# The tokens of an inverse 47-point transform as 64x47 products on four quarters of TensorE, in place of 128x94 products on the whole array

## The chip, the cores and the metric

The kernel runs on one core of one Trainium2 chip. The metric is the device time of one execution in microseconds (us). Three runs of the kernel before took 2612.84 to 2614.05 us, with a median of 2612.94 us. The profiled execution is another one, of 2617.29 us; its span, which every view below is read against, is 2615.5 us.

## The reference

Eight sequences of 3008 rows by 256 channels go through a real Fourier transform along the rows, a complex linear layer with bias, a soft threshold, and the inverse transform. The 24064 resulting rows ("tokens") go through a feed-forward network of 256 to 2048 to 256 channels with a sigmoid-gated activation.

```python
X = np.fft.rfft(x, axis=1)
Yr = Xr @ w_r - Xi @ w_i + b_r
Yi = Xr @ w_i + Xi @ w_r + b_i
Yr = np.sign(Yr) * np.maximum(np.abs(Yr) - lam, 0.0)
Yi = np.sign(Yi) * np.maximum(np.abs(Yi) - lam, 0.0)
y = np.fft.irfft(Yr + 1j * Yi, n=x.shape[1], axis=1)
...
h = x @ w_in
g = h * (1.0 / (1.0 + np.exp(-1.702 * h)))
return (g @ w_out).astype(np.float32)
```

## The kernel before

The length 3008 is 64 x 47, so each transform is done as products with a 64-point and a 47-point matrix. For one sequence, `dft47` (or `stage_a`) applies the 47-point step, `dft64` (in `stage_b`) the 64-point step, `stage_mix` the linear layer, `threshold` the soft threshold, and `stage_inv` the inverse 64-point step. The result lies in DRAM as the tile `s2`, of shape [48, 2, 32, 256]: 24 frequencies times real and imaginary part, then `p` (0 or 1: even and odd rows of the transform), then 32 columns `j`, then 256 channels.

What is left is the inverse 47-point step, and this is what the change touches. `load_u(u)` (L525) brings two columns `j` of `s2` into an SBUF tile `ur` of 96 partitions: the 48 values of p = 0 and the 48 of p = 1 lie interleaved in the partitions. `tokens(u)` (L533) multiplies it: the stationary operand is a 96x128 piece of `ur` (one column, one half of the channels), the moving operand is the constant `kz`, 96x94. `kz` holds the 47-point matrix twice, once for each p, with zeros where the p of the row and the p of the column differ. Four products (two columns, two channel halves) fill one PSUM tile `pa` with 2 x 188 columns: 188 tokens by 256 channels. `split` (L147) then writes it out twice: ScalarE casts it to a rounded high part `th`, and VectorE subtracts this from the PSUM tile to get the low part `tl`. There are 16 such groups for a sequence, 128 in all. A tile `th`, `tl` holds 512 tokens; a group that crosses a border of 512 is split in two pieces.

All these products are FP32. TensorE carries each out as two pairs of a weight load and a matmul, so the 512 products of `tokens` stand as 1024 weight loads and 1024 matmuls in the trace. The products of the feed-forward network are in a rounded format (fp32r), where each factor is a high and a low part and three products stand for one (`mm3`, L156): each of those is one load and one matmul.

The feed-forward network takes 512 tokens at a time (47 blocks). `Ffn.up(q)` makes the hidden values of 256 of the 2048 units (12 matmuls of 128x512), `down(q)` the output sums (21 matmuls of 128x256, a seven-product scheme), each over eight values of q. While the blocks run, the spectral steps of the next sequences are emitted between them in step with a cost count, and `tokens_to` (L618) emits `tokens` shortly before a block needs them. It loads one group ahead.

A scheduler then orders the instructions of each engine, and each engine takes its own in that order. The buffers that matter here: `bank()` hands out four PSUM tiles `pa`, used by `tokens`, `up`, `dft64`, `stage_mix` and the other spectral steps alike; `buf2` hands out seven SBUF tiles under one tag, used by `ur` and by nearly all intermediate tiles of the spectral steps and of the output. DMA starts of these tiles are issued on the queue of SyncE (SP).

One more place of the kernel before matters for reading the trace: in the first sequence, `stage_inv` (inside `first_batch`) multiplies with stationary operands on 64 partitions, those of i = 0 on partitions 0 to 63 and those of i = 1 on partitions 64 to 127, each 64x128, with 256 moving columns and an output tile `pi` for each i:

```python
for r in range(2):
    for i in range(2):
        hs = slice(64 * i, 64 * i + 64)
        mm(po[i][:, h], st[r][hs], v[hs, r], start=r == 0, stop=r == 1)
```

Of the kernel before, what the change touches and what calls it, by code (L numbers as in the profile page):

```python
# [9 lines left out]
F32 = mybir.dt.float32  # L10
# [9 lines left out]
S, N1, N2 = 3008, 64, 47  # L20
D, DFF = 256, 2048
LAM = 0.01
NS = 24
NJ = N1 // 2
JP = 2 * 2 * N2
NU = NJ // 2
TOK, HT = 512, 256
NQ = DFF // 256
W2 = 7
WARM = 3  # L30
PK, PKR = 618, 822
TINY = float(np.uint32(897 << 20).view(np.float32))


# [5 lines left out]
def halves(v):  # L40

    def r12(u):
        m, e = np.frexp(u)
        return np.ldexp(np.rint(m * 4096.0), e - 12)

    hi = r12(v)
    return hi, r12(v - hi)


def constants():  # L50
    def ang(a, b, n):
        return 2.0 * np.pi * ((np.outer(a, b)) % n) / n

    n1, n2, k1, k2 = np.arange(N1), np.arange(N2), np.arange(N1), np.arange(NS)
    t47 = ang(n2, k2, N2)
    t64 = ang(n1, k1, N1)


    fa = np.zeros((48, NS, 2))
    fa[:N2, :, 0] = np.cos(t47)  # L60
    fa[:N2, :, 1] = -np.sin(t47)
    a = np.kron(fa.reshape(48, 48), np.eye(2))


    sign = np.ones((N1, NS))
    for kk2 in range(1, NS):
        for kk1 in range(N1):
            k = next(k for k in range(kk2, S, N2) if k % N1 == kk1)
            sign[kk1, kk2] = 1.0 if k <= S // 2 else -1.0


    c, s = np.cos(t64), np.sin(t64)
    b = np.stack([np.block([[c, -s * sign[:, k]], [s, c * sign[:, k]]]) for k in range(NS)])
    b = b.reshape(NS // 2, 2, 2 * N1, 2 * N1).transpose(0, 2, 1, 3)


    w0r, w0i = np.zeros(N1), np.zeros(N1)
    for kk1 in range(N1):
        if next(k for k in range(0, S, N2) if k % N1 == kk1) <= S // 2:
            edge = kk1 in (0, N1 // 2)  # L80
            w0r[kk1] = (1.0 if edge else 2.0) / S
            w0i[kk1] = 0.0 if edge else 2.0 / S
    ct, st = c.T, s.T
    inv = np.block([[ct, st], [-st, ct]])
    binv = inv * (2.0 / S)
    binv0 = inv * np.concatenate([w0r, w0i])[:, None]
    binv0[:, N1:] = 0.0


    ai = np.zeros((NS, 2, 2, 2, N2))  # L90
    for p in range(2):
        ai[:, 0, p, p] = np.cos(t47.T)
        ai[:, 1, p, p] = -np.sin(t47.T)
    ai = ai.reshape(96, 94)

    packs = np.zeros((128, PKR), np.float32)
    packs[:96, 0:192] = np.concatenate(halves(a), 1)
    packs[:, 192:704] = np.concatenate([h[i] for h in halves(np.stack([binv, binv0])) for i in range(2)], 1)
    packs[:96, 704:798] = ai
    packs[:, 798:822] = 1.0  # L100
    packs[N1:, 798:822] = sign

    kinv = np.stack([binv[:N1], binv[N1:]], 1)
    kfirst = np.concatenate([np.stack([binv0[:N1], binv0[N1:] * sign[:, :1]], 1),
                             np.stack([binv[:N1], binv[N1:] * sign[:, 1:2]], 1)])
    pack = np.zeros((128, PK), np.float32)
    pack[:, 0:256] = np.tile(kinv, (2, 1, 1)).reshape(128, 256)
    pack[:, 256:512] = kfirst.reshape(128, 256)
    pack[:, 512:524] = sign.T.reshape(NS // 2, 2 * N1).T
    pack[:96, 524:618] = ai  # L110
    plain = np.zeros((128, 128), np.float32)
    plain[:96, 0:96] = a
    return np.concatenate([plain, np.eye(128, dtype=np.float32), pack, packs], 1), b.astype(np.float32)
# [3 lines left out]
def fourier_mix_then_gated_ffn(ctx: ExitStack, tc: tile.TileContext, x, w_r, w_i, b_r, b_i, w_in, w_out, pack, kbs, out):  # L117
    nc = tc.nc
    NB = x.shape[0]
    NT = out.shape[0]  # L120
    a96, eye, pack, packs = pack[:96, 0:128], pack[:, 128:256], pack[:, 256:256 + PK], pack[:, 256 + PK:256 + PK + PKR]
# [10 lines left out]
    def bank():  # L132
        return ps_a.tile([128, 512], F32, name="pa", tag="pa")

    def buf(shape, dt, name, tag=None, bufs=2):
        return wk.tile(shape, dt, name=name, tag=tag or name, bufs=bufs)

    def buf2(name):
        return buf([128, 2, D], F32, name, tag="w2", bufs=W2)

    def after(*keys):
        held = ExitStack()
        for k in keys:
            held.enter_context(tc.issue_after(done_at[k]))
        return held

    def split(hi, lo, src):  # L147
        nc.scalar.copy(hi, src)  # L148
        return nc.vector.tensor_tensor(lo, src, hi.bitcast(F32), ALU.subtract)  # L149
# [3 lines left out]
    def mm(ps, w, t, start=True, stop=True):  # L153
        last[0] = nc.tensor.matmul(ps, lhsT=w, rhs=t, start=start, stop=stop).ins  # L154
# [9 lines left out]
    def const(shape, dt, name):  # L164
        return cst.tile(shape, dt, name=name, tag=name.rstrip("_"))

    ka = const([96, 128], F32, "ka")
    ki = const([128, 512], F32, "ki")
    kz = const([96, 94], F32, "kz")
    fg = const([128, NS], F32, "fg")  # L170
    bias = const([128, 2, D], F32, "bias")
    wf = const([128, 3, 2, D], F32, "wf")
# [2 lines left out]
    parts, done_at = {}, {}  # L175
# [9 lines left out]
    def constants_in():  # L185
        nc.sync.dma_start(ki, pack[:, 0:512])
        nc.sync.dma_start(fg[:, 0:12], pack[:, 512:524])
        nc.sync.dma_start(kz, pack[:96, 524:618])
        nc.sync.dma_start(bias[:, 0], b_r.broadcast_to([128, D]))
        nc.sync.dma_start(bias[:, 1], b_i.broadcast_to([128, D]))  # L190
        with after(("w", 0)):
            nc.vector.tensor_scalar(bias, bias, LAM, None, ALU.subtract)
# [7 lines left out]
                nc.vector.scalar_tensor_tensor(wf[:, i], wf[:, 2], -1.0, wi, ALU.mult, op)  # L200

    def rounded_parts():
        pk = buf([128, 822], F32, "pk", tag="sx", bufs=3)
        nc.sync.dma_start(pk, packs)
        parts["a"] = const([96, 2, 96], F32R, "ka_")
        parts["i"] = const([128, 2, 2, 128], F32R, "ki_")
        parts["f"] = const([128, NS], F32, "fg_")
        nc.scalar.copy(parts["a"].rearrange("p a b -> p (a b)"), pk[:96, 0:192])
        nc.scalar.copy(parts["i"].rearrange("p h z n -> p (h z n)"), pk[:, 192:704])
        nc.scalar.copy(parts["f"], pk[:, 798:822])  # L210
        wr, wi = buf2("wr"), buf2("wi")
        for t, w in ((wr, w_r), (wi, w_i)):
            nc.sync.dma_start(t, w.rearrange("(c p) e -> p c e", p=128))
        parts["h"] = const([128, 3, 2, D], F32R, "wf_h")
        parts["l"] = const([128, 3, 2, D], F32R, "wf_")
        split(parts["h"][:, 2], parts["l"][:, 2], wr)
        for i, op in ((0, ALU.add), (1, ALU.subtract)):
            t = buf2("wd")
            nc.vector.scalar_tensor_tensor(t, wr, -1.0, wi, ALU.mult, op)
            split(parts["h"][:, i], parts["l"][:, i], t)  # L220
# [302 lines left out]
    s2s, us, ytiles = {}, {}, {}  # L523

    def load_u(u):  # L525
        b, jp = divmod(u, NU)
        if b < NB and u not in us and b in s2s:
            t = buf2("ur")[:96]
            s2v = s2s[b].rearrange("c p j d -> (c p) j d")
            nc.sync.dma_start(t, s2v[:, 2 * jp:2 * jp + 2])  # L530
            us[u] = t

    def tokens(u):  # L533
        t = us.pop(u)
        pv = bank()[:, :2 * JP].rearrange("p (c n) -> p c n", c=2)
        for c in range(2):
            for j in range(2):
                mm(pv[:, c, 94 * j:94 * j + 94], t[:, j, 128 * c:128 * c + 128], kz)
        lo = JP * u
        while lo < JP * (u + 1):  # L540
            k, at = divmod(lo, TOK)
            n = min(JP * (u + 1) - lo, TOK - at)
            if k not in ytiles:
                ytiles[k] = (fbuf([128, 2, TOK], F32R, "th"), fbuf([128, 2, TOK], F32R, "tl"))
            th, tl = ytiles[k]
            o = lo - JP * u
            split(th[:, :, at:at + n], tl[:, :, at:at + n], pv[:, :, o:o + n])
            lo += n

    def fbuf(shape, dt, name, bufs=2):  # L550
        return ff.tile(shape, dt, name=name, tag=name, bufs=bufs)
# [66 lines left out]
    def tokens_to(n):  # L618
        nonlocal done
        while done < NB * NU and JP * done < n:  # L620
            load_u(done)
            load_u(done + 1)
            tokens(done)
            done += 1
        load_u(done)
# [41 lines left out]
    for q in range(8):  # L667
        with after(("i", 5)):
            dft47(1, q, x1[q // 2][:, 2 * (q % 2):2 * (q % 2) + 2])
        if q == 1:  # L670
            for u in range(3):
                load_u(u)
    for n in (7, 8):
        with after(("v", 11)):
# [23 lines left out]
    for n in range(NT * NQ):  # L698
        k, q = divmod(n, NQ)
# [10 lines left out]
        elif not queue and nextb < NB:  # L710
# [4 lines left out]
            total, spent, n0 = sum(c for c, _ in queue), 0.0, n  # L715
            n1 = NQ * S * nextb // TOK - 12
            nextb += 1
        while queue and spent < total * (n + 1 - n0) / (n1 - n0):
            c, step = queue.pop(0)
# [46 lines left out]
```

## Time and profile before

| | value |
|---|---|
| median of three runs | 2612.94 us |
| the profiled execution | 2617.29 us |
| its span | 2615.5 us |
| ScalarE (ACT) busy | 1635.6 us, 63% |
| VectorE (DVE) busy | 1983.4 us, 76% |
| matmuls of `tokens` (`pa<-kz,ur`) | 1024, first at 105.6 us, last at 2541.3 us |
| weight loads of the whole program | 16711 |
| loads of `ur` from DRAM | 128, 192 KB each, median 3.0 us from issue to landing |
| DMA over the span | 214.16 MB, mean 82 GB/s |

How to read the views. PE is TensorE's matmuls, PEld its weight loads, which run beside matmuls; the recorded duration of a matmul includes its way through the array, so what a matmul costs in a dense stretch is read from the distance between starts, not from its duration. A row of a timeline gives the start in us, the duration in us, the engine, the line, the operation, the output and input tiles, the form of the array (rows*columns in use), the shape of the operand, and how many like instructions were merged. All matmuls go through the helper `mm` and stand at L154, so they are told apart by their tiles. A row of waits gives who waited for whom, the total in us, how often, and the longest.

### The profile page before, as it was taken

To read this page: it belongs to the slowest core of one execution; us is meant where nothing else is said; L and a number is where in the kernel's file an instruction comes from. 1 tells how busy PE (TensorE), PEld (TensorE's weight loads), DVE (VectorE), ACT (ScalarE), POOL (GpSimd) and SP (SyncE) were. 2 spreads that over 40 slices of the span, in tenths; PEclk is the share of its full clock that TensorE was granted. 3 is DMA by queue.
4 is the path that set the end of the run, shared out by engine and by line. 5 is a ranking of instruction groups with operands and counts; after the bars stand their busy time and mean duration, and the time that the engine had idled before them with its cause. 6 is when DMAs were issued, how large, how long until landed. Compare 5 with 4: busy or idle time off the path is not lost. (4 is left out here: it accounts for less than half of the span.)

```text
span 2615.5 us, 42827 instructions
## 1 busy us (share of the span) xinstructions
PE 2585.2 (99%) x16711; PEld 2334.6 (89%) x16711; DVE 1983.4 (76%) x3214; ACT 1635.6 (63%) x2536; POOL 56.8 (2%) x66
## 2 busy tenths in 40 slices
PE   8999999999999999999999999999999999999998
PEld 7669999999899998999989999899998899999997
DVE  6688777787778777787777877777777787777776
ACT  4566665666766667666676666766666566655554
POOL 0000000000000000000000000000000000000000
PEclk9999999999999999999999999999999999999999
DMA  6553331222322224222242222322223132200000
GB/s 189 158 173 91 90 105 56 58 72 61 110 77 74 84 69 129 64 81 81 72 131 65 82 72 82 119 61 84 81 85 116 46 95 74 79 24 26 18 20 17
DMA packets 168396, 214.16 MB, mean 82 GB/s; under 512 B 16368, under 2 KB 119120, under 8 KB 168192
## 3 DMA queue, kind: packets, MB, share of 16 engines
q1 hardware_dynamic: 166144, 204.00, 26.4%
q0 software_dynamic: 2048, 7.41, 1.0%
q8 instruction: 132, 2.16, 0.4%
q14 instruction: 72, 0.59, 0.1%
HBM read 117.49 MB, written 93.85 MB: 81 GB/s over the span
## 5 line engine op out<-in xcount | busy, mean ns | idle before, releaser
L572 ACT ACTIVATE gb<-pa 128x512 f32<-128x512 f32 x752 | 448.3, 597 | 447.9 <-PE pa L154 445.6
L149 DVE TENSOR_TENSOR lt<-gt,ht 128x1024 fp32r<-128x1024 f32 x376 | 465.9, 1239 | 248.9 <-ACT ht L148 248.3
L154 PE MATMUL pa<-th,wi_h 128*128 128x512 f32 x1504 | 593.6, 395 | 0.5 <-ACT th L148 0.5
L154 PE MATMUL pa<-tl,wi_h 128*128 128x512 f32 x1504 | 591.8, 394 | 0.0
L154 PE MATMUL pa<-th,wi_l 128*128 128x512 f32 x1504 | 588.4, 391 | 0.0
L148 ACT CAST ht<-gt 128x1024 fp32r<-128x1024 f32 x376 | 393.8, 1047 | 153.0 <-DVE gt L583 151.9
L154 PE MATMUL po<-lt,wo_h 128*128 128x256 f32 x1504 | 411.8, 286 | 0.6 <-DVE lt L149 0.6
L154 PE MATMUL po<-ht,wo_l 128*128 128x256 f32 x1504 | 407.9, 284 | 0.0
L149 DVE TENSOR_TENSOR lb<-gb,hb 128x768 fp32r<-128x768 f32 x376 | 361.5, 961 | 27.7 <-ACT hb L148 25.0
L581 DVE TENSOR_TENSOR gt<-gb 128x512 f32<-128x512 f32 x376 | 259.3, 690 | 159.6 <-ACT gb L572 152.2
L154 PE MATMUL po<-ht,wo_h 128*128 128x256 f32 x1504 | 360.2, 284 | 1.6 <-ACT ht L148 1.4
L154 PEld LDWEIGHTS pa<-th,wi_l 128*128 128x128 f32 x1504 | 283.7, 189 | 56.3
L148 ACT CAST hb<-gb 128x768 fp32r<-128x768 f32 x376 | 314.4, 836 | 22.8 <-PE po L154 15.6
L154 PEld LDWEIGHTS pa<-th,wi_h 128*128 128x128 f32 x1504 | 284.8, 189 | 44.9 <-ACT th L148 0.7
L154 PEld LDWEIGHTS pa<-tl,wi_h 128*128 128x128 f32 x1504 | 284.9, 189 | 41.1
L154 PE MATMUL po<-lb,wo_h 128*128 128x256 f32 x1128 | 317.9, 285 | 2.1 <-DVE lb L149 2.1
L154 PE MATMUL po<-hb,wo_l 128*128 128x256 f32 x1128 | 315.6, 283 | 0.0
L154 PE MATMUL po<-hb,wo_h 128*128 128x256 f32 x1128 | 313.6, 291 | 0.0
L154 PEld LDWEIGHTS po<-lt,wo_h 128*128 128x128 f32 x1504 | 286.3, 190 | 10.7 <-issue 1.6
L154 PEld LDWEIGHTS po<-ht,wo_l 128*128 128x128 f32 x1504 | 286.1, 191 | 8.6 <-issue 2.5
L154 PEld LDWEIGHTS po<-ht,wo_h 128*128 128x128 f32 x1504 | 262.3, 190 | 11.9 <-ACT ht L148 1.6
L154 PEld LDWEIGHTS po<-lb,wo_h 128*128 128x128 f32 x1128 | 214.3, 190 | 10.4 <-DVE lb L149 2.2
(102 smaller groups left out, 3591.6 us busy)
## 6 DMA issues: line engine op xcount, KB each, us to landing
s<-iev SPq DMA_DIRECT2D x96, 256.0 KB, 2.2
ur<-s SPq DMA_DIRECT2D x128, 192.0 KB, 3.0
out<-o SPq DMA_DIRECT2D x94, 256.0 KB, 2.2
s<-aev SPq DMA_DIRECT2D x112, 192.0 KB, 2.3
br<-s SPq DMA_DIRECT2D x84, 256.0 KB, 3.0
yd<-mv SPq DMA_DIRECT2D x168, 128.0 KB, 2.4
yr<-yd SPq DMA_DIRECT2D x84, 256.0 KB, 3.0
xr<-in_x SPq DMA_DIRECT2D x104, 192.0 KB, 3.1
```

Of the source, the lines that this page charges most:

```text
L148: nc.scalar.copy(hi, src)
L149: return nc.vector.tensor_tensor(lo, src, hi.bitcast(F32), ALU.subtract)
L154: last[0] = nc.tensor.matmul(ps, lhsT=w, rhs=t, start=start, stop=stop).ins
L572: done_at["g"] = nc.scalar.activation(o, ps.rearrange("p (h n) -> p h n", h=2), AF.Gelu_apprx_sigmoid).ins
L581: nc.vector.tensor_tensor(gt[:, 0:2], b12, gb[:, 0:3:2], ALU.subtract)
```

## The change

The two values of p no longer share a product. The constant `kz` becomes the bare 48x47 matrix, held twice, on partitions 0 to 47 and 64 to 111. A group has four columns j in place of two (64 groups in place of 128), and its input is two `ur` tiles, each with two columns; p = 0 lies on partitions 0 to 47 and p = 1 on 64 to 111, so each tile is loaded by two DMAs of 96 KB. A product has a stationary operand of 48 partitions by 64 channels and 47 moving columns; its place in the array follows from the partitions of its input (the half of the rows, p) and of its output (the half of the columns, the channel block c modulo 2). Four products in a row thus lie on the four quarters. A group is 32 products and fills two PSUM tiles, one for each p, of 376 columns. On TensorE the order of the group's products among themselves is fixed by hand. The outputs are written to `th` and `tl` with a stride, since each PSUM tile has runs of 47 tokens that alternate with those of the other one; a column that crosses a border of 512 tokens is written in pieces of its own.

```diff
-JP = 2 * 2 * N2
-NU = NJ // 2
+JP = 4 * 2 * N2
+NU = NJ // 4
...
-    ai = np.zeros((NS, 2, 2, 2, N2))
-    for p in range(2):
-        ai[:, 0, p, p] = np.cos(t47.T)
-        ai[:, 1, p, p] = -np.sin(t47.T)
-    ai = ai.reshape(96, 94)
+    ai = np.stack([np.cos(t47.T), -np.sin(t47.T)], 1).reshape(48, N2)
...
-    kz = const([96, 94], F32, "kz")
+    kz = const([128, N2], F32, "kz")
...
     def load_u(u):
         b, jp = divmod(u, NU)
         if b < NB and u not in us and b in s2s:
-            t = buf2("ur")[:96]
-            s2v = s2s[b].rearrange("c p j d -> (c p) j d")
-            nc.sync.dma_start(t, s2v[:, 2 * jp:2 * jp + 2])
-            us[u] = t
+            s2v = s2s[b].rearrange("c p j d -> p c j d")
+            us[u] = [buf2("ur") for h in range(2)]
+            for h, t in enumerate(us[u]):
+                for p in range(2):
+                    nc.sync.dma_start(t[64 * p:64 * p + 48], s2v[p, :, 4 * jp + 2 * h:4 * jp + 2 * h + 2])
 
     def tokens(u):
-        t = us.pop(u)
-        pv = bank()[:, :2 * JP].rearrange("p (c n) -> p c n", c=2)
-        for c in range(2):
-            for j in range(2):
-                mm(pv[:, c, 94 * j:94 * j + 94], t[:, j, 128 * c:128 * c + 128], kz)
-        lo = JP * u
-        while lo < JP * (u + 1):
-            k, at = divmod(lo, TOK)
-            n = min(JP * (u + 1) - lo, TOK - at)
+        ts = us.pop(u)
+        pv = [bank()[:, :JP].rearrange("p (c j n) -> p c j n", c=2, j=4) for p in range(2)]
+        with tc.manual_schedule(engines={mybir.EngineType.PE}):
+            for j in reversed(range(4)):
+                for c in range(4):
+                    i = 64 * (c % 2)
+                    for p in reversed(range(2)):
+                        hs = slice(64 * p, 64 * p + 48)
+                        mm(pv[p][i:i + 64, c // 2, j], ts[j // 2][hs, j % 2, 64 * c:64 * c + 64], kz[hs])
+        for k in range(JP * u // TOK, (JP * (u + 1) - 1) // TOK + 1):
             if k not in ytiles:
                 ytiles[k] = (fbuf([128, 2, TOK], F32R, "th"), fbuf([128, 2, TOK], F32R, "tl"))
             th, tl = ytiles[k]
-            o = lo - JP * u
-            split(th[:, :, at:at + n], tl[:, :, at:at + n], pv[:, :, o:o + n])
-            lo += n
+            at = [JP * u + 94 * j - TOK * k for j in range(4)]
+            js = [j for j in range(4) if 0 <= at[j] and at[j] + 94 <= TOK]
+            for p in range(2):
+                if js:
+                    hi, lo = (t[:, :, at[js[0]]:at[js[0]] + 94 * len(js)].rearrange("p c (j n) -> p c j n", j=len(js))[:, :, :, 47 * p:47 * p + 47]
+                              for t in (th, tl))
+                    split(hi, lo, pv[p][:, :, js[0]:js[0] + len(js)])
+                for j in range(4):
+                    a = at[j] + 47 * p
+                    n0, n1 = max(0, -a), min(47, TOK - a)
+                    if j not in js and n0 < n1:
+                        split(th[:, :, a + n0:a + n1], tl[:, :, a + n0:a + n1], pv[p][:, :, j, n0:n1])
...
-            for u in range(3):
+            for u in range(2):
                 load_u(u)
```

How the scheduler's order moves is shown at two places. The first is TensorE in the middle of the program, where matmuls of the feed-forward network (`po` of `down`, `pa<-th,wi_h` of `up`) stand around a group of `tokens` (`pa<-kz,ur`); `[waits ...]` names the queues and engines whose semaphores a row waits for. In the kernel before:

```order
L154 MATMUL po_7137<-ht,wo_l 128x256
L154 MATMUL po_7139<-lt,wo_h 128x256
L154 MATMUL pa<-kz,ur 128x94 [waits DMAHW4_49,DVE_49]
L154 MATMUL pa<-kz,ur 128x94 x3
L154 MATMUL po_7139<-ht,wo_l 128x256
L154 MATMUL pa<-th,wi_h 128x512 [waits PE_49,Activation_49]
```

The same engine at a group of the changed kernel:

```order
L150 MATMUL po_7739<-ht,wo_h 128x256
L150 MATMUL pa<-kz,ur 64x47 [waits DMAHW3_49,Activation_49]
L150 MATMUL po_7737<-lt,wo_h 128x256 [waits DVE_49]
L150 MATMUL po_7737<-ht,wo_l 128x256
L150 MATMUL pa<-kz,ur 64x47 [waits DMAHW2_49,Activation_49]
L150 MATMUL pa<-kz,ur 64x47 x14
L150 MATMUL pa<-kz,ur 64x47 [waits DMAHW1_49]
L150 MATMUL pa<-kz,ur 64x47 [waits DMAHW0_49]
L150 MATMUL pa<-kz,ur 64x47 x14
L150 MATMUL po_7738<-lt,wo_h 128x256
```

Four products of one group became 32 of one group (for twice the tokens), with a wait for each of its four loads and for each of its two PSUM tiles. The order of the 32 among themselves is fixed, but other matmuls may stand between them: here the first product stands alone, two matmuls of `down` follow, and then the other 31. Over the program the 64 groups stand in 134 uninterrupted runs of quartered products; 71 cuts go through a group, most of them behind its first product, and two groups at the start stand in one run.

The second place is ScalarE at the first block, where `th<-pa` are the casts of `tokens` and `gb<-pa` is the first activation of the feed-forward network. Before:

```order
L148 CAST th<-pa 128x2x188
L409 COPY aev<-pa 96x512
L148 CAST th<-pa 128x2x188
L148 CAST th<-pa 128x2x136
L148 CAST th<-pa 128x2x52
L572 ACTIVATE gb<-pa 128x2x256
```

In the changed kernel:

```order
L144 CAST th<-pa 128x2x4x47 x2
L144 CAST th<-pa 128x2x47 x2
L144 CAST th<-pa 128x2x2x47
L144 CAST th<-pa 128x2x42
L144 CAST th<-pa 128x2x47
L144 CAST th<-pa 128x2x2x47
L144 CAST th<-pa 128x2x5
L580 ACTIVATE gb<-pa 128x2x256
```

Two groups of 376 tokens stand where three of 188 stood, and the second one, which crosses a border of 512, is written in seven pieces. Over the program the 174 casts of `tokens` become 314, and so do the subtractions of VectorE; the 128 DMA starts of `ur` on SP become 256.

More of the change, by code (lines that the diff above doesn't have):

```diff
@@ L30 @@
 WARM = 3
-PK, PKR = 618, 822
+PK, PKR = 571, 728
 TINY = float(np.uint32(897 << 20).view(np.float32))
@@ L98, in constants @@
     packs[:, 192:704] = np.concatenate([h[i] for h in halves(np.stack([binv, binv0])) for i in range(2)], 1)
-    packs[:96, 704:798] = ai
-    packs[:, 798:822] = 1.0
-    packs[N1:, 798:822] = sign
+    packs[:, 704:728] = 1.0
+    packs[N1:, 704:728] = sign
     kinv = np.stack([binv[:N1], binv[N1:]], 1)
@@ L109, in constants @@
     pack[:, 512:524] = sign.T.reshape(NS // 2, 2 * N1).T
-    pack[:96, 524:618] = ai
+    for p in range(2):
+        pack[64 * p:64 * p + 48, 524:571] = ai
     plain = np.zeros((128, 128), np.float32)
@@ L187, in constants_in @@
         nc.sync.dma_start(fg[:, 0:12], pack[:, 512:524])
-        nc.sync.dma_start(kz, pack[:96, 524:618])
+        nc.sync.dma_start(kz, pack[:, 524:571])
         nc.sync.dma_start(bias[:, 0], b_r.broadcast_to([128, D]))
@@ L202, in rounded_parts @@
     def rounded_parts():
-        pk = buf([128, 822], F32, "pk", tag="sx", bufs=3)
+        pk = buf([128, PKR], F32, "pk", tag="sx", bufs=3)
         nc.sync.dma_start(pk, packs)
@@ L209, in rounded_parts @@
         nc.scalar.copy(parts["i"].rearrange("p h z n -> p (h z n)"), pk[:, 192:704])
-        nc.scalar.copy(parts["f"], pk[:, 798:822])
+        nc.scalar.copy(parts["f"], pk[:, 704:728])
         wr, wi = buf2("wr"), buf2("wi")
@@ L545, in tokens @@
             th, tl = ytiles[k]
-            o = lo - JP * u
-            split(th[:, :, at:at + n], tl[:, :, at:at + n], pv[:, :, o:o + n])
-            lo += n
+            at = [JP * u + 94 * j - TOK * k for j in range(4)]
+            js = [j for j in range(4) if 0 <= at[j] and at[j] + 94 <= TOK]
+            for p in range(2):
+                if js:
[7 more added lines that the diff above has]
+                        split(th[:, :, a + n0:a + n1], tl[:, :, a + n0:a + n1], pv[p][:, :, j, n0:n1])
     def fbuf(shape, dt, name, bufs=2):
```

## The prediction

> **What bounds the kernel now.** I read the page's busy shares and granted clock first, then the waits, to see who waits for whom.
>
> ```profile
> PE 2585.2 (99%) x16711; PEld 2334.6 (89%) x16711; DVE 1983.4 (76%) x3214; ACT 1635.6 (63%) x2536; POOL 56.8 (2%) x66
> PEclk9999999999999999999999999999999999999999
> ```
>
> ```profile
> PE pa L154 <- DMA ur<-s: 3.6, 1, 3.6
> ...
> ACT gb L572 <- PE pa L154: 445.6, 489, 3.8
> ```
>
> TensorE works for the whole span at full clock. The longest of its own waits in total is 3.6 us, once, at the first group of `tokens`; ScalarE waits for TensorE 489 times, VectorE is idle for 24% of the span. So the time is what TensorE's instructions take, one behind the other, and a saving or an addition there goes into the end one to one. Next: what `tokens` takes there, from its groups and from the timeline around one of them, matmuls first, then weight loads.
>
> ```profile
> L154 PE MATMUL pa<-kz,ur x1024: 242/275/496, 105.6 to 2541.3; 96*128 96x94 f32 x171
> ```
>
> ```profile
> 652.73 0.28 PE L154 MATMUL pa<-wf_h,zz 128*128 128x256 f32 x1
> 652.85 1.03 PE L154 MATMUL pa<-kz,ur 96*128 96x94 f32 x8
> 653.66 0.36 PE L154 MATMUL po<-hb,wo_h 128*128 128x256 f32 x1
> 653.86 0.28 PE L154 MATMUL po<-lb,wo_h 128*128 128x256 f32 x1
> 653.98 0.28 PE L154 MATMUL po<-hb,wo_l 128*128 128x256 f32 x1
> ```
>
> ```profile
> 652.73 0.98 PEld L154 LDWEIGHTS pa<-kz,ur 96*128 96x128 f32 x8
> 653.63 0.19 PEld L154 LDWEIGHTS po<-hb,wo_h 128*128 128x128 f32 x1
> ```
>
> Durations overlap, so I count starts. From the first of the eight at 652.85 to the second matmul behind them at 653.86 are 1.01 us; without the group that second one would start one slot of 0.12 us later (653.86 to 653.98). The group costs 0.89 us. Its eight loads stand 652.73 to 653.63, 0.90 us or 0.112 us each: **the loads set the pace**, not the 94 columns.
>
> **What goes.** 128 groups x 0.89 = **113.9 us**, 4.4% of the span.
>
> **What comes: rounds.** 64 groups x 32 products x 2 = 4096 pairs of load and matmul. If each quarter works by itself, that is 64 x 16 = 1024 rounds of four: as many as there were pairs before, each with a load of 64 columns instead of 128. Do parts of the array work at once? `pi` in the first sequence shows it for the two halves of the rows. Matmuls first, then loads:
>
> ```profile
> 78.00 0.39 PE L154 MATMUL pa<-k,rows 128*128 128x128 f32 x2
> 78.32 0.49 PE L154 MATMUL pi<-mv,ki 64*128 64x256 f32 x2
> 78.64 0.38 PE L154 MATMUL pi<-mv,ki 64*128 64x256 f32 x2
> 78.86 0.38 PE L154 MATMUL pi<-mv,kt 64*128 64x256 f32 x2
> 79.07 0.38 PE L154 MATMUL pi<-mv,kt 64*128 64x256 f32 x2
> 79.39 0.38 PE L154 MATMUL pa<-k,rows 128*128 128x128 f32 x1
> ```
>
> ```profile
> 78.12 0.28 PE L154 MATMUL pa<-k,rows 128*128 128x128 f32 x1
> ```
>
> ```profile
> 78.32 0.19 PEld L154 LDWEIGHTS pi<-mv,ki 64*128 64x128 f32 x2
> 78.43 0.19 PEld L154 LDWEIGHTS pi<-mv,ki 64*128 64x128 f32 x2
> ```
>
> Matmuls start in pairs, one on each half, 0.215 us from pair to pair (78.64, 78.86, 79.07); loads too, two at 78.32 and two at 78.43, two loads of 128 columns in 0.11 us. So row halves load and multiply at once. That column halves do, no row here shows. Per pair, 256 columns take 0.215 us, so 47 take 0.040 us; a round is then set by its load. How long is one of 64 columns? The recorded durations fall with the columns:
>
> ```profile
> L154 PEld LDWEIGHTS pa<-k,rows 128*128 128x128 f32 x96 | 12.2, 192 | 2.5 <-ACT rows L353 1.0 <-issue 1.0 <-DVE w L277 0.3
> L154 PEld LDWEIGHTS pa<-xr,ka 96*96 96x96 f32 x48 | 7.1, 165 | 6.8 <-ACT ht L148 3.1 <-issue 2.5 <-ACT aev L409 0.4
> ```
>
> 32 columns fewer are 27 ns less, so 64 fewer take 54 ns off 0.112: **0.056 us**, to which I hold. Bounds: 0.040 (the matmul alone) and 0.112 (loads don't shrink). With column halves in turn it is 2 x 0.056.
>
> **What comes: turns of the array.** The same rows show what it costs to go to halves and back. In: `k,rows` starts every 0.12 us, the last at 78.12; `pi` loads at 78.32, 0.09 late against its slot, and nothing was loaded ahead, so the first load lies open (it is the first round, counted above). Out: the last pair starts at 79.07 and streams 0.215, to 79.285; the next load starts at 79.39, 0.10 later, and takes 0.11 before its matmul goes. With 47 columns: 0.04 + 0.10 + 0.11 = 0.25 from the last quartered product. A turn in and out costs 0.09 + 0.25 = 0.34, with the stagger of four quarters 0.345 us. Another visit agrees on the way in:
>
> ```profile
> 83.53 0.28 PE L154 MATMUL pa<-k,rows 128*128 128x128 f32 x1
> 83.73 0.70 PE L154 MATMUL pi<-mv,ki 64*128 64x256 f32 x4
> ```
>
> In the order, quartered products stand in 134 uninterrupted runs, since 71 cuts go through groups: 134 x 0.345 = **46.2 us**. A lone product takes two rounds that its group doesn't save elsewhere: 1024 + 2 x 71 = 1166 rounds x 0.056 = **65.3 us**. Bounds: turns from 0 (the array needn't empty for quarters) to 0.40 (with a load of 128 columns on the way in too); rounds as above.
>
> **What else moves.** Each of the 140 added casts and subtractions costs at least its fixed part, the shortest of its kind:
>
> ```profile
> L148 ACT CAST th<-pa x174: 156/449/484, 108.1 to 2541.7; 128x376 fp32r<-128x376 f32 x82, 128x272 fp32r<-128x272 f32 x2, 128x104 fp32r<-128x104 f32 x2, 128x168 fp32r<-128x168 f32 x2
> L149 DVE TENSOR_TENSOR tl<-pa,th x174: 154/522/552, 108.6 to 2542.2; 128x376 fp32r<-128x376 f32 x82, 128x272 fp32r<-128x272 f32 x2, 128x104 fp32r<-128x104 f32 x2, 128x168 fp32r<-128x168 f32 x2
> ```
>
> 140 x 0.155 = 22 us on each, hidden by their idle 37% and 24%; a price stands under the rivals. The elements stay the same; the stride in the output I take as free (no row has it). SP starts 256 loads of `ur` instead of 128, of half the size:
>
> ```profile
> ur<-s SPq DMA_DIRECT2D x128, 192.0 KB, 3.0
> ```
>
> They are issued a group ahead, and a group now lasts twice as long, some 40 us (64 in 2430), against 3.0 us to landing: hidden. The first block needs two groups with eight loads instead of three with three; I put this at nothing, within 1 us either way.
>
> **The sum.** 113.9 - 65.3 - 46.2 = 2.4 us less. The profiled execution took 2617.29 us (span 2615.5), so 2614.9; it lies 4.35 us above the median of the runs shown, so 2610.5. **Forecast: 2610 us**, no change that a measurement of this kernel can tell from none (0.2%, 5.2 us). Rounds of 0.050 to 0.062 and turns of 0.31 to 0.38 move it by 8 us, to 2602 and 2618.
>
> **Rivals.**
>
> *Column halves in turn (slower).* Two quarters that share rows take their loads one behind the other: 1166 rounds become 2332, 65 us more, **2675 us**. It decides from the moment that a second load into the same rows waits for the first. For it: only row halves are seen at once. Against it: on the whole array, the load at 652.73 starts with the matmul of that start, in the same rows, so a shared row alone blocks nothing. Chance 0.15. The Trainium skill, "TensorE: Matmul & The Clock Gate", Part 3, has weight loads overlap matmuls in flight only when the row group differs. By that rule this rival comes true; the rows at 652.73 speak against its wording, and its section also lists a 16-tile packing with both splits at 10.6 times the speed, which speaks for the quarters.
>
> *Quarters cost less than read (faster).* Turns at half their price, 23 us less, or rounds at the matmul's 0.040, 19 us less: about **2589 us**, or 2568 if both. For it: the rows of `pi` have a load of 128 columns in every turn and 256-column products to empty; a lone 47-column product may leave sooner. Against it: both turns above show the same distance to 0.01 us. Chance 0.28.
>
> *PSUM tiles and small pieces (slower).* A group holds two of the four `pa` tiles until up to seven pieces are written, and ScalarE and VectorE do them in order among longer work. If every group makes TensorE wait for one cast of 0.45 us, that is 29 us; at a third of them 10: **2620 to 2639 us**. It decides once a tile comes free later than the matmul that needs it. Against it: ScalarE waits for TensorE, not the reverse. Chance 0.09.
>
> *A floor per instruction (slower).* 4096 pairs might not be fed in 0.014 us each. At 0.025 per pair they take 102 us instead of 65: **2647 us**; above 0.014 it starts to decide. The rows of `pi` show two loads and two matmuls at 78.32 within 0.01 us, though only in a burst. Chance 0.04. The Trainium skill, same page, "Wait — 56ns, not 53.3ns?", gives about 25 ns from start to start for small matmuls; the two at 78.32 lie closer.
>
> **How the numbers follow.** Forecast 0.44, split by its 8 us: 0.17 faster, 0.22 within 0.2%, 0.05 slower. Cheaper quarters 0.28, all faster. In turn 0.15 and the floor 0.04, all slower. Pieces 0.09: 0.01 within, 0.08 slower. Together faster 0.45, same 0.23, slower 0.32. The range goes from 2578 (most of the cheaper quarters) to 2678 (column halves in turn); it leaves out both halves of the cheaper case together, and loads that don't shrink at all (0.112 a round, also 2675 alone, more with turns in sequence). The forecast's own range is 2602 to 2618.
>
> **What would show it.** In the changed profile: 4096 loads and matmuls of `pa<-kz,ur`, form 48*64; starts in fours, 0.056 us from four to four, and a group of 32 from first load to next full matmul in some 1.2 us. In fours at 0.11: column halves in turn. A load 0.09 to 0.10 us behind the end of the stream before and behind each run: the turns. If TensorE's waits for casts of `th` or for VectorE stay under 5 us, the pieces cost nothing; if its busy share falls under 98%, they do. Wrong would be: fewer runs than 134 in the trace, rounds that no longer keep the four together, or time that lies outside of the `kz` products and their neighbours.

## The result and the profile after

The changed kernel takes **2650.12 us** (median, 2648.87 to 2652.06) against 2612.89 for the kernel before; ratio 1.0144, 95% interval 1.0131 to 1.0156. It is 37 us slower; the forecast was 2610, the range 2578 to 2678. The page of the changed kernel, busy shares and granted clock:

```profile
PE 2594.2 (98%) x19783; PEld 2304.1 (87%) x19783; DVE 1988.7 (75%) x3354; ACT 1641.0 (62%) x2676; POOL 55.5 (2%) x66
PEclk9899999999999999999999999999999999999999
```

TensorE is busy 98% of a longer span: it waits now. First, are the quarters what was forecast? The timeline around one group, matmuls and then loads (start, duration, count):

```profile
638.64 0.39 PE L150 MATMUL pa<-th,wi_l 128*128 128x512 f32 x1
638.96 1.15 PE L150 MATMUL pa<-kz,ur 48*64 48x47 f32 x64
640.03 0.38 PE L150 MATMUL po<-hb,wo_h 128*128 128x256 f32 x1
640.25 0.28 PE L150 MATMUL po<-lb,wo_h 128*128 128x256 f32 x1
640.37 0.28 PE L150 MATMUL po<-hb,wo_l 128*128 128x256 f32 x1
```

```profile
638.95 1.02 PEld L150 LDWEIGHTS pa<-kz,ur 48*64 48x64 f32 x64 [0.35 <-issue]
```

and the view of the tile, with the least, median and longest duration in ns:

```profile
L150 PEld LDWEIGHTS pa<-kz,ur x4096: 128/135/229, 106.4 to 2561.5; 48*64 48x64 f32 x196
```

64 loads last 1.02 us from the first start to the last end, and one lasts 0.135: 15 steps from four to four in 0.885 us, 0.059 each. All four quarters work at once. Without the group the matmul of 640.25 would start two slots behind 638.64 (0.23 and 0.12, 638.99); the group costs 1.26 us, as 16 rounds and one turn say (1.24).

So the time is elsewhere. The longest waits of TensorE (total, times, longest):

```profile
PE pa L150 <- ACT xh L144: 13.0, 6, 3.7
PE pa L150 <- issue: 6.0, 1, 6.0
PE pa L150 <- ACT aev L405: 3.9, 2, 2.3
```

The six waits for `xh`, the cast of a piece of x, stand at five of the borders between two sequences (near 690, 1015, 1340, 1665 and 1985 us, two of them at the first; the expectations below count six borders). The chain of waits at one of them (start, duration, what, pieces between left out):

```profile
1332.42 3.38 DMA s<-iev
...
1335.88 0.32 SPq L528
...
1336.25 0.42 SPq L528
...
1336.71 0.42 SPq L528
...
1337.17 0.42 SPq L528
...
1337.64 2.93 DMA xr<-in_x
...
1340.60 0.63 ACT xh L144
...
1341.27 0.74 PE pa L150
```

and SP's timeline at that border in the changed kernel, then in the kernel before:

```profile
1326.24 6.54 SPq L497 DMA_DIRECT2D s<-iev  x4
1335.88 1.72 SPq L528 DMA_DIRECT2D ur<-s  x4
1337.64 5.30 SPq L425 DMA_DIRECT2D xr<-in_x  x5
```

```profile
1313.33 2.87 SPq L501 DMA_DIRECT2D s<-iev  x2
1316.24 0.95 SPq L429 DMA_DIRECT2D xr<-in_x  x2
1321.00 0.38 SPq L501 DMA_DIRECT2D s<-iev  x1
1321.49 0.89 SPq L429 DMA_DIRECT2D xr<-in_x  x2
1324.76 0.31 SPq L530 DMA_DIRECT2D ur<-s  x1
```

SP starts its transfers in order. L528 is the load of `ur`, and the first group of the new sequence reads what the last `iev` wrote, so its four starts wait until those writes have landed. Behind them stand the `xr` loads of the next sequence. The first of these waits for nothing else: it starts 0.05 us behind the last start of `ur`. In the kernel before, `xr` stood ahead.

To see where each kernel's time goes I summed its matmul starts in the profiled execution: a *kz run* costs from the matmul ahead of it to the second one behind, less those two slots; a *gap* is what lies between two other starts beyond the first one's slot (0.230 us at 512 columns, 0.1195 at 256, 0.112 at 128). The first run holds the wait for the first `ur`.

| us | before | after | difference |
|---|---|---|---|
| kz runs but the first | 111.6 | 108.1 | -3.5 |
| first kz run | 10.1 | 13.2 | +3.1 |
| gaps to 200 us | 55.5 | 56.6 | +1.1 |
| gaps from 200 us on | 3.6 | 36.4 | +32.8 |
| span | 2615.5 | 2649.0 | +33.5 |

Not all of the 36.4 us is waiting. From 200 us on, the waits that the profile lists for TensorE come to 23.6 us (4.1 before). The granted clock fell too. Here are 200 us around the border above (busy times of the engines, granted clock, share and GB/s of the DMA), the changed kernel first:

```profile
1200.00:1400.00 200.00, 196.17 (x1488) 174.31 (x1487) 148.01 (x250) 129.91 (x217) 3.13 (x3) 0.98 0.33 94
```

```profile
1200.00:1400.00 200.00, 200.00 (x1282) 180.65 (x1281) 152.88 (x246) 133.85 (x213) 4.72 (x4) 1.00 0.31 94
```

The clock was 1.00 from 1330 to 1340 us and 0.50 from 1340.5 to 1347.3. Behind the wait of 3.7 us, matmuls of 256 columns then start 0.21 us apart in place of 0.12. Each of the five borders has such a stretch, 23.9 us in all; the kernel before has one of 3.4 us from 200 us to its last block. The matmuls that start in these stretches take some 8 us more than their slots, against 1 before (estimates, from the starts). So a wait at a border cost more than its own length.

### The profile page after: what moved, and what is told of

The parts are those of the page before. It is cut to its first block, busy times and chain, and to the rows that moved or that the text cites. A ratio compares the mean times of both kernels' runs of the same rounds, so it can differ in the third digit from the quotient of the medians.

```text
span 2649.0 us, 49417 instructions
## 1 busy us (share of the span) xinstructions
PE 2594.2 (98%) x19783; PEld 2304.1 (87%) x19783; DVE 1988.7 (75%) x3354; ACT 1641.0 (62%) x2676; POOL 55.5 (2%) x66
## 4 chain that ended last, share of the span: by engine, by line
PE 91%; DMA 4%; DVE 2%; ACT 1%; issue 1%; SPq 0%; ACTq 0%; DVEq 0%; POOLq 0%
PE pa L150 56%; PE po L150 35%; DMA xr<-in_x 1%; DMA s<-aev 1%; DMA yr<-yd 1%; DMA wraw<-in_w_out 0%; DMA s<-iev 0%; PE pi L150 0%; DMA wraw<-in_w_in 0%; DMA xh<-in_x 0%; SPq L528 0%; ACT ht L144 0%; DVE lt L145 0%; DMA bias<-in_b_i 0%; DMA ur<-s 0%
## 5 line engine op out<-in xcount | busy, mean ns | idle before, releaser
L150 PE MATMUL po<-ht,wo_h 128*128 128x256 f32 x1504 | 349.5, 285 | 1.9 <-ACT ht L144 1.9
L144 ACT CAST hb<-gb 128x768 fp32r<-128x768 f32 x376 | 314.4, 837 | 23.6 <-PE po L150 15.5
L150 PE MATMUL po<-hb,wo_h 128*128 128x256 f32 x1128 | 302.9, 290 | 4.1 <-ACT hb L144 2.6
L150 PEld LDWEIGHTS po<-ht,wo_h 128*128 128x128 f32 x1504 | 258.4, 190 | 14.5 <-ACT ht L144 2.9
L150 PEld LDWEIGHTS po<-hb,wo_h 128*128 128x128 f32 x1128 | 210.4, 190 | 23.9 <-ACT hb L144 4.7
```

## The experiments

Every ratio is to the kernel before, run beside it on the same chip; its median was 2613.8 to 2614.9 there. "Gaps" are those from 200 us on.

| run | us | ratio (95%) | kz runs: count, us but the first | gaps |
|---|---|---|---|---|
| e1 | 2631.72 | 1.0071 (1.0054-1.0087) | 133, 107.7 | 14.3 |
| e2 | 2626.92 | 1.0050 (1.0035-1.0065) | 134, 108.0 | 20.6 |
| e3 | 2657.78 | 1.0171 (1.0156-1.0187) | 97, 110.9 | 44.2 |
| e4 | 2646.19 | 1.0122 (1.0107-1.0138) | 145, 112.9 | 38.0 |
| e5 | 2646.95 | 1.0125 (1.0110-1.0140) | 122, 103.1 | 36.6 |
| e6 | 2627.93 | 1.0049 (1.0034-1.0064) | 122, 103.5 | 16.9 |
| e7 | 2638.44 | 1.0095 (1.0080-1.0110) | 135, 108.5 | 19.8 |
| e8 | 2615.67 | 1.0001 (0.9989-1.0013) | 80, 85.8 | 26.1 |
| e9 | 2619.15 | 1.0020 (1.0010-1.0029) | 93, 111.8 | 4.5 |
| e10 | 2640.93 | 1.0105 (1.0089-1.0120) | 223, 142.0 | 3.0 |
| e11 | 2616.96 | 1.0013 (1.0004-1.0023) | 159, 114.9 | 3.9 |
| e12 | 2618.76 | 1.0016 (1.0007-1.0026) | 75, 84.4 | 30.6 |
| e13 | 2620.99 | 1.0027 (1.0015-1.0039) | 124, 106.0 | 14.5 |
| e14 | 2604.89 | 0.9958 (0.9942-0.9975) | 78, 86.7 | 14.8 |
| e15 | 2613.64 | 0.9995 (0.9986-1.0005) | 73, 83.6 | 26.5 |
| e16 | 2618.17 | 1.0017 (1.0007-1.0026) | 97, 110.2 | 4.0 |
| e17 | 2612.30 | 0.9992 (0.9983-1.0001) | 145, 112.4 | 3.0 |
| e18 | 2612.88 | 0.9992 (0.9983-1.0001) | 91, 91.9 | 16.2 |

### Four theories: e1 to e4

The expectation of e1 names the four theories. "w2 buffers" are the seven tiles of `buf2`.

**e1**, `xr` ahead of `ur` on SP (`whole` holds the sequences whose steps are all written, at first only 0):

```diff
-        if b < NB and u not in us and b in s2s:
+        if u not in us and b in whole:
...
+        if queue:
+            load_u(done)
         need = TOK * (1 + (n + 2) / NQ)
...
             tokens_to(need)
+        if not queue:
+            whole.add(nextb - 1)
```

> The changed kernel, but the `ur` loads of a new sequence's first group are written one step later, so that on SP the first `xr` loads of the next sequence stand ahead of them. Groups of four columns, quarters, the earlier emptying of the list of spectral steps, the seven w2 buffers and the turns of the array all stay (133 runs instead of 134). Theory 1 (SP's queue: `xr` stands behind `ur` loads that wait for the last writes of s2): the stalls at six sequence borders go, 34 us less than 2650, so 2612 to 2622, ratio to before 1.000 to 1.004. Theory 2 (too few w2 buffers, since two `ur` tiles are held per group): unchanged, 2643 to 2655. Theory 3 (the spectral steps are emptied earlier and all at once, need + JP with JP = 376): unchanged, 2643 to 2655. Theory 4 (the quartered products themselves cost 34 us more than read): unchanged, 2643 to 2655.

2631.72 us: 18 less than the changed kernel, half the loss. SP's timeline of e1 at the same border shows the edit at work:

```profile
1312.32 5.53 SPq L497 DMA_DIRECT2D s<-iev  x3
1317.89 0.95 SPq L425 DMA_DIRECT2D xr<-in_x  x2
1318.94 0.38 SPq L497 DMA_DIRECT2D s<-iev  x1
1319.44 1.95 SPq L425 DMA_DIRECT2D xr<-in_x  x2
1326.17 0.31 SPq L441 DMA_DIRECT2D s<-aev  x1
1326.52 0.43 SPq L529 DMA_DIRECT2D ur<-s  x1
```

The gaps fall from 36.4 to 14.3 us; the rest of what theory 1 promised (2612 to 2622) isn't there.

**e2**, `ur` on another queue:

```diff
-                    nc.sync.dma_start(t[64 * p:64 * p + 48], s2v[...])
+                    nc.gpsimd.dma_start(t[64 * p:64 * p + 48], s2v[...])
```

> The changed kernel, but the four loads of `ur` per group are issued by GpSimd in place of SP; nothing else is edited. Theory 1: `xr` has nothing of `ur` ahead of it on SP, so the stalls at the borders go: 2612 to 2625, where the upper end is for `ur` landing later from GpSimd's queue. Theories 2, 3 and 4: 2643 to 2655, since buffers, emptying and products are the same.

2626.92 us: 23 less, a little above theory 1's range. With nothing moved but the queue, most of the loss goes; theories 2 and 4 cannot give that.

**e3**, groups of four without quarters:

```diff
-JP = 2 * 2 * N2
-NU = NJ // 2
+JP = 4 * 2 * N2
+NU = NJ // 4
...
-            t = buf2("ur")[:96]
-            nc.sync.dma_start(t, s2v[:, 2 * jp:2 * jp + 2])
-            us[u] = t
+            us[u] = [buf2("ur")[:96] for h in range(2)]
+            for h, t in enumerate(us[u]):
+                nc.sync.dma_start(t, s2v[:, 4 * jp + 2 * h:4 * jp + 2 * h + 2])
```

> The kernel before, with its 96x128 by 94 products on the whole array, its casts and its turns (none), but with groups of four columns (JP = 376): two loads of `ur` per group right behind one another, two tiles held. No quarter in it. Theory 1: its SP order also has both `ur` loads ahead of the next `xr` loads at every border, with two starts of 0.43 us instead of four: stalls of some 5 us instead of 6 at six borders, 2635 to 2646. Theory 2 and 3: as slow too, 2635 to 2650 (they differ from theory 1 in the other runs). Theory 4: no loss, 2610 to 2616.

2657.78 us, above every forecast: larger groups alone lose 44 us, with no quarter in the kernel. Theory 4 falls.

**e4**, the kernel before, emptied early:

```diff
-        while queue and need + JP > S * (nextb - 1):
+        while queue and need + 2 * JP > S * (nextb - 1):
```

> The kernel before with one edit: the list of spectral steps is emptied when need + 2 * JP passes the border, as early as in the changed kernel. SP's order keeps the `xr` loads ahead of the `ur` load of the new sequence. Theory 1 and 4: 2610 to 2617, no stall at the borders. Theory 3: most of the 34 us, 2635 to 2650. Theory 2: 2610 to 2617.

2646.19 us: theory 3's range, in a kernel with one `ur` load per group. Is that a second mechanism? SP's timeline at a border of e4:

```profile
1323.78 8.29 SPq L501 DMA_DIRECT2D s<-iev  x3
1332.13 0.46 SPq L530 DMA_DIRECT2D ur<-s  x1
1332.63 0.44 SPq L429 DMA_DIRECT2D xr<-in_x  x1
1333.17 0.38 SPq L501 DMA_DIRECT2D s<-iev  x1
1333.65 1.45 SPq L429 DMA_DIRECT2D xr<-in_x  x3
```

Emptied early, three writes of s2 hold SP for 8.29 us, as they wait for their `iev` (the copies out of PSUM), and `xr` stands behind them. That reads as SP's queue again, with another transfer at its head; e4 wasn't tried with those writes on another queue.

### Which of the two edits counts: e5 to e7

**e5** is the changed kernel with `need + 188` for `need + JP` (and `load_u` allowed once the list is empty), `ur` still ahead; **e6** is e1 with `need + 188`; **e7** the changed kernel with `nc.gpsimd` in the one line that loads `xr`.

> The changed kernel with the spectral steps emptied as late as in the kernel before (need + 188 instead of need + 376), and the `ur` loads of the new sequence still ahead of its neighbours' `xr` loads on SP. With the run e1 (early emptying, xr ahead: 2632) and the changed kernel (early, ur ahead: 2650) this makes a square of two edits. If only the emptying counted: 2612 to 2618. If the two costs add (18 for ur ahead, the rest for the early emptying): 2628 to 2635. If only the place of ur counted, the same 2628 to 2635 with stalls before `xh,ka` at the borders; if neither, 2645 to 2655. 122 uninterrupted runs of quartered products instead of 134 are worth 5 us less in each case.

> Both edits together: emptied late, and `xr` ahead of `ur` on SP, in the changed kernel with its quarters. If the order of the work at the borders explains the whole loss: the prediction's own sum returns, 2610 less 5 us for 122 runs instead of 134: 2603 to 2613. If the quartered products cost something that the sum doesn't have: above 2625.

> The changed kernel with one edit: the `xr` loads of the spectral steps are issued by GpSimd, so that on their way to the DMA they have neither the writes of s2 nor the loads of ur ahead of them. Emptying stays early, and the order of the other queues close to as it was. If SP's queue is the cause of both parts of the loss: 2612 to 2622. If the early emptying costs by itself (ScalarE and VectorE get five steps at once): 2628 to 2635. If the w2 buffers are the cause (an `xr` tile has to wait for the buffer of an `iev` whose write to s2 isn't done): 2643 to 2655, with GpSimd's `xr` starts waiting for those writes instead of SP's.

e5 2646.95, e6 2627.93, e7 2638.44. The square: with `ur` ahead, emptying late is worth 3 us (2650 to 2647); with `xr` ahead, 4 (2632 to 2628); `xr` ahead is worth 18 and 19. In the changed kernel it is the place of `ur` that counts, and the early emptying hardly does. By its ranges e5 says "neither"; but the range given there for the place of `ur` alone was set wrong, since e5 leaves `ur` ahead and so could gain nothing by it. e7 lies above its range for the early emptying and below that for the w2 buffers, though its gaps fall to 19.8: its span also ends 4 us later behind the last matmul (10.0 us from its start to the end, 6.0 in the changed kernel). Its `xr` tiles come from the same seven buffers, so buffers alone (theory 2) don't explain the gaps. e6 still lies 13 us over the kernel before, above the 2603 to 2613 that the prediction's sum gave it.

### Fewer turns: e8, e10 to e12

The cuts through groups stand in the order of the program. As read from it, a group's first product finds a free `pa` tile, and the second tile comes free later. **e8** is e6 with

```diff
-        with tc.manual_schedule(engines={mybir.EngineType.PE}):
+        opened = nc.vector.memset(pv[0][:, 0, 0, 0:1], 0.0).ins
+        with tc.issue_after(opened), tc.high_priority(), \
+             tc.manual_schedule(engines={mybir.EngineType.PE}):
```

**e12** has the same edit on e1. **e10** is the changed kernel with JP = 188, 128 groups of two columns and two `ur` loads each; **e11** is e10 with e8's edit.

> The kernel of e6 with its groups held together: VectorE first writes one column of the first `pa` tile, so that no product starts before both tiles are free, and the products get a higher priority in the order. 80 uninterrupted runs instead of 122. By the prediction's price of a turn (0.345 us) with two rounds of 0.058 for a lone product, 42 x 0.46 = 19 us less than e6: 2585 to 2596. If turns cost nothing (the time of the runs lies elsewhere): as e6. If the earlier place in the order makes TensorE wait for casts instead: above e6.

> Quartered products, but in groups of two columns like the kernel before (JP = 188, 128 groups, two loads of `ur` each), so that the groups keep their places. 223 uninterrupted runs of kz products: 223 x 0.345 = 77 us of turns, and 1024 + 2 x 95 rounds of 0.0585 = 71 us, together 148 against the 122 of the kernel before: 26 us more, 2640, if the price of a turn holds. If turns are cheaper than read: 2615 to 2630. If the extra casts and subtractions (more than in the changed kernel) cost 16 us on top: 2650 to 2662.

> The kernel of e10 with the groups held together as in e8: 159 runs, 159 x 0.345 = 55 us, 1024 + 66 rounds of 0.0585 = 64 us, 119 in all: 3 us less than the kernel before, 2611, and 29 us less than e10. If extra casts and subtractions cost 16 us on top: 2622 to 2630. If turns are cheaper than read, it lies closer to e10 than 20 us.

> The run e1 (groups of four, early emptying, `xr` ahead; 2632 with 133 runs) with the groups held together: 75 runs. By the price of a turn 58 x 0.46 = 27 us less than e1: 2600 to 2610. e8 got 12 of the 19 us that 42 runs less should have brought; if waits take the place of the rest here too, 2612 to 2620.

e10: 2640.93, forecast 2640, which is in part luck. The forecast set 148 us of kz runs against 122, and the 122 holds the wait of the first run, while the 148 does not; without that wait the same prices give some 2650. In the sums the runs but the first cost 142.0 us against 111.6, 30 more, and the gaps of the first 200 us are 6 fewer; those behind are 3.0, fewer than before too. So quarters in the old groups lose by their 223 turns, and by no new gaps. e11: 24 us less than e10 for 64 runs less, 0.37 us a run by the times and (142.0 - 114.9) / 64 = 0.42 in the sums, with the rounds that a lone product wastes; the level is 6 us above its forecast, which used the same 122. e8 and e12 save the turns (18 and 23 us of kz time against e6 and e1) but give 9 and 16 back in gaps. So e8 misses its 2585 to 2596 by 20 us, and e12 comes out in its range for waits in the place of turns.

### The rest of the loss: e9, e13, e16

**e9** is e3 with e6's two edits. **e13** is e6 with `ur` on GpSimd (e2's edit). In e6 SP's timeline has the loads of a group ahead of a `yr` load within a sequence too:

```profile
1229.58 2.07 SPq L529 DMA_DIRECT2D ur<-s  x3
1231.75 0.37 SPq L618 DMA_DIRECT2D out<-o  x1
1232.17 0.42 SPq L529 DMA_DIRECT2D ur<-s  x1
1232.68 0.38 SPq L476 DMA_DIRECT2D yr<-yd  x1
```

**e16** is e9 with both `pa` tiles held through a group and every cast and subtraction halved.

> The run e3 (no quarters, groups of four columns on the whole array; 2658) with the two edits of e6: emptied late, `xr` ahead of `ur` on SP. It has the 174 casts and subtractions of the kernel before, no turns, and groups as large as the changed kernel's. What is left of e6's loss (2628 against 2614, where the sum said 2603 to 2613) comes either from larger groups, which deal the fixed order of all engines anew (then this kernel loses too: 2622 to 2640), or from the 140 extra casts and subtractions of the quarters (then it doesn't: 2610 to 2617). In both cases it is at least 15 us below e3, if SP's order is what e1 and e6 say.

> The kernel of e6 (emptied late, `xr` ahead; 2628) with its `ur` loads issued by GpSimd. In e6 the four `ur` starts of a group, 2.07 us for three and 0.42 us behind an `out` write, stand ahead of a `yr` load within a sequence too, and TensorE waits for `yh` and then `gb` behind that. If SP's queue is the rest of the loss: 2608 to 2616. If tiles and pieces are: 2622 to 2630, as e6.

> The kernel of e9 (whole array, groups of four, both edits; 2619) with the quarters' way with tiles put into it: the products go to the two `pa` tiles in turn, so that both are held until the whole group is done, and each cast and subtraction is done in two halves (348 of each in place of 174). No quarter, no turn. If held tiles and pieces are the rest of e6's loss: 2629 to 2640. If not: 2616 to 2622.

e9: 2619.15, between its two ranges and 39 us below e3, gaps 44.2 to 4.5: without quarters the two edits mend larger groups almost wholly. e16: 2618.17, gaps 4.0: tiles held longer and twice the pieces cost nothing there. e13: 2620.99, between its two ranges. Of its 7 us the records put 3.4 into the first kz run (13.6 to 10.2) and 4.9 into the gaps of the first 200 us (58.5 to 53.6), but only 2.4 into those behind. So SP's queue held up the first block as well, and the `yr` loads behind `ur` are not the cause of most gaps within sequences. **Open:** 11 us of gaps (14.5 against 3.6 before) that quarters in groups of four have and that neither e9 (fours) nor e10 (quarters) shows. In e13's trace the listed waits of TensorE from 200 us on come to 9.4 us against 4.1 before; all are for ScalarE and VectorE, none is longer than 1.8 us. What makes those late isn't shown. That e16 stands for what the quarters do with tiles is argued, not shown, as it has no quarters.

### A version faster than both: e14, e15, e17, e18

**e14** and **e15** are e8 and e12 with `ur` on GpSimd, **e17** the kernel before with that edit alone, **e18** is e14 without the priority.

> The kernel of e8 (e6 with uncut groups; 2616) with its `ur` loads issued by GpSimd, 78 runs. If SP's queue is the rest: 2596 to 2604, faster than both kernels. If tiles and pieces are: 2610 to 2620.

> The kernel of e12 (emptied early, uncut groups; 2619) with its `ur` loads issued by GpSimd, 73 runs. If SP's queue is the rest: 2597 to 2606, with the early emptying worth nothing by itself, as e5 says. If tiles and pieces are, or if the early emptying costs here: 2612 to 2620.

> The kernel before with one edit: its single `ur` load per group is issued by GpSimd. If SP's queue costs the kernel before nothing, as its waits read (no wait of over 1 us at a border): 2609 to 2619, and e14's gain is that of the uncut quarters. If the queue change is what made e14 fast: 2600 to 2608.

> The kernel of e14 without the higher priority of the kz products; VectorE's opening column stays. 91 runs instead of 78: 13 x 0.42 = 5 us more by the price of a turn, 2608 to 2613. If the priority is what costs TensorE waits: 2595 to 2603.

e14: **2604.89 us, 0.9958 (0.9942 to 0.9975)**, 9 us faster than the kernel before and 45 faster than the changed one; one of its four executions took 8528.1 us, so the ratio rests on three. Its tile of kz products against that of the changed kernel (busy us and mean ns; idle ahead), the changed kernel first:

```profile
L150 PE MATMUL pa<-kz,ur 48*64 48x47 f32 x4096 | 96.1, 237 | 7.5 <-issue 6.0 <-ACT aev L405 1.6
```

```profile
L150 PE MATMUL pa<-kz,ur 48*64 48x47 f32 x4096 | 79.5, 236 | 4.8 <-DMA ur<-s 4.8
```

The same 4096 matmuls cover 16.6 us less of the span in 78 runs than in 134. e17 shows no change (0.9992, interval to 1.0001), so the queue alone isn't e14's gain. e15 has 26.5 us of gaps and comes out even, in the upper of its ranges: there, with the early emptying, the gaps eat what the turns save. e18 is 8 us slower than e14 with 13 runs more and gaps of 16.2, so the priority isn't what causes the gaps.

## Why the prediction was wrong

- **What bounds the kernel: right.** TensorE has no slack: 32.8 us of new gaps became 33.5 us of span. The "full clock" that the prediction read there held only until TensorE waited: part of the gaps is its clock at half (0.50) behind the waits.
- **What goes and what comes: right.** Rounds were forecast at 0.056 us (the step that it takes off, 0.112 - 0.054, gives 0.058) and measured at 0.059; a group at some 1.2 us and measured at 1.26. The kz runs but the first cost 3.5 us less than before, forecast 2.4. In e10 both prices give 148 us for 223 runs, and the sums have 142.0 for all but the first.
- **Column halves in turn: didn't happen.** Quarters that share rows load at once (0.059 us for four, not 0.11). The Trainium skill, "TensorE: Matmul & The Clock Gate", Part 3, has weight loads overlap matmuls in flight only when the row group differs; this trace disagrees for column halves, and the measurement decides.
- **A floor per instruction: didn't happen** down to 0.059 / 4 = 0.015 us a pair.
- **PSUM tiles and small pieces:** its upper end, 2639, came near the time, but the waits are for `xh` behind a DMA, and e16, without quarters, shows no price.
- **The step that failed:** "They are issued a group ahead, and a group now lasts twice as long [...]: hidden." The landing was hidden; the *starts* were not. The step counted how long a load has until its own group needs it, and not what waits behind it on SP. The load of a new sequence's first group waits for the last writes of s2, and four starts of it (1.72 us) and that wait (3.38) stand ahead of `xr`. Putting `xr` ahead takes 18 (e1) and 19 us (e6 against e5) off a loss of 37.
- **A smaller miss:** "The first block [...] I put this at nothing, within 1 us either way". The first kz run takes 3.1 us more, which goes when `ur` leaves SP (e2: 10.1, e13: 10.2).

What remains is the open 11 us above. The prediction had named the sign of its own failure, time outside of the kz products and their neighbours; it gave that case no price. That 2650 lies within 2578 to 2678 is luck: the upper part of the range was set by column halves in turn, which didn't happen.

## What to carry to other kernels

Where one engine issues transfers in order, a load that waits for data also delays every load behind it: when a change regroups work, read the queue's order at the borders, where a producer's last write is awaited, and not only the lead of the loads that changed. When the bounding engine has no slack, the price of an edit is its own work plus every wait that the new order makes, and here plus the slower clock behind a wait; try the edit without the regrouping (e10) and the regrouping without the edit (e3) to price them apart.

## What the hardware showed beyond that

Four quarters of 48 rows by 64 columns take their loads and 47-column matmuls at once, 0.059 us from four to four. Counted by starts, a run of 32 matmuls costs 0.80 us (e10) and one of 64 costs 1.27 (the changed kernel): 0.058 a round of four, which leaves 0.34 us for going to quarters and back. With the rounds that a lone product wastes it is 0.42; with 78 turns instead of 134 the quarters cost 86.7 us where the whole array takes 111.6, which is what e14 gains, less 11 us of gaps (span 2603.0 against 2615.5).
